# A fused spectral filter and token MLP: natural order in the first middle unit, the first token tile ahead, and MLP product tiles that open as banks come free

## The chip, the cores and the metric

The kernel runs on one core of a Trainium2 chip. The metric is device time in microseconds (us) of one execution; lower is better. PE is TensorE, DVE is VectorE, ACT is ScalarE, SP is the synchronising engine, which issues the transfers. PSUM is the memory that the matrix products write to; the kernel uses it in eight banks. A *hole* is time in which TensorE stands still and waits.

## The reference, cut to what matters

```python
def _layernorm(x, axis=-1, eps=1e-5): ...

def _A_ref(x, w_r, w_i):                       # global spectral filter
    X = rfft2(x.astype(float32), axes=(-2, -1)) * (w_r + 1j * w_i)
    return irfft2(X, s=(S, D)).astype(bfloat16)

def _B_ref(x, w1, b1, w2, b2):                 # MLP over the tokens
    u = gelu(einsum("bsd,sf->bdf", _layernorm(x), w1) + b1)
    return (einsum("bdf,fs->bds", u, w2) + b2).transpose(0, 2, 1)

h  = A_x + _A_ref(_layernorm(A_x), A_w_r, A_w_i)
h2 = h + _B_ref(_layernorm(h), B_w1, B_b1, B_w2, B_b2)   # S=2048, D=512, F=1376, bf16
```

## The kernel before

All Fourier transforms are matrix products. The program has three stages on TensorE. First come the forward products. In the middle, eight "units" each mix rows, multiply by the filter weights on DVE (`v`, tile `V`), and start the inverse. Last come 16 token tiles: inverse products `g2`, a copy from PSUM by ACT (`eo`, tile `EO`), the transform `g3`, three adds on DVE (`tl`, `th`, `h`, tiles `TT` and `H`), a square and a reciprocal root on ACT (`q`, `r2`, tiles `JK` and `r`), and a normalised tile on DVE (`hh`, tile `HH`). The first MLP layer has 11 product tiles of 16 products each, one for every token tile: `mm1_t_s2` needs `hh_s2`. The second layer (`mm2`) and the final adds follow, and need all of the first.

The order of the instructions and the use of the eight PSUM banks are made by a list scheduler inside the program when it is built. An operation takes part in the order by its readiness and its priority; lists called FRONT force the order of some. A group of matmuls that share a bank is a unit of a class; each class has a limit of open banks, and a unit that is not `early` may take a bank only when all its inputs are ready.

```python
FRONT = {
    "dve": """bn_0 ag_0 ... fs_13 fs_14 fs_15 ys_12 ys_14""",           # cut
    "act": """rs_0 fs_0 ... ys_11 ys_13 yh_150 yh_151""",               # cut
    ...}
K = Builder(nc, {"f1": 7, "f2": 2, "x": 2, "g1": 2, "g2": 2, "g3": 2, "mm1": 5, "mm1b": 6, "mm2": 8})
...
            if not u.early and any(remaining[x.idx] > inner[x.idx] for x in u.ops if x.pw):
                continue                                     # wait until all inputs are ready
...
def mm1(t, s2):
    Mt = NP if t < 10 else 96
    if t not in w1units:
        w1units[t] = PsumUnit("mm1" if t < 5 else "mm1b", 1, early=t < 5)
    mm(f"mm1_{t}_{s2}", lambda bank: ps[0:Mt, bank, :], W1[:, s2, t * NP:t * NP + Mt], HH[:, s2, :], w1units[t],
       s2 == 0, s2 == NS2 - 1, s2 == 0, 2 if t < 5 else 1, 512)

for s2 in range(NS2):
    unit = PsumUnit("g2", 1)
    ...                                                      # g2, eo, g3, tl, th, h, q, r2, hh
    for t in range(5):
        mm1(t, s2)
```

So in the kernel before only five product tiles can be worked on while tokens still arrive; the sixth may open only when all 16 normalised tiles exist. (In the built order just one product of the sixth stands ahead of the last token tile's first product.)

## Time and profile before

| | before |
|---|---|
| time, median of the 3 runs known when the prediction was made (lowest to highest); 133.91 with a fourth | 133.87 us (133.81 to 134.03) |
| profiled span | 132.2 us |
| PE busy | 123.3 us, 93% of the span |
| first token tile's MLP product | 45.88 us |
| last token tile's first MLP product | 69.03 us |
| last matmul starts | 128.48 us |
| from there to the end of the span | 3.69 us |

How to read it: from the last token tile on, TensorE has all its inputs and runs at its own rate, so the end is set by how much work is left when that tile arrives. Every first-layer product done earlier, in a hole, comes off the end with 0.216 us. The lines of the profile are in the prediction below.

### The profile page before, as it was taken

How to read it: one execution, taken by the hardware profiler on the slowest of the kernel's cores; microseconds unless marked ns; L12 is line 12 of the kernel's file. 1: busy time of each engine (PE TensorE's matmuls, PEld its weight loads, DVE VectorE, ACT ScalarE, POOL GpSimd, SP SyncE). 2: the span in 40 equal slices, each digit the busy share in tenths (PEclk: the TensorE clock that was granted, in tenths of full speed). 3: DMA queues.
4: the chain of work that ended last, by engine and by line, in shares of the span. 5: the costliest groups of instructions: out<-in, count | busy, mean ns of one | idle time of the engine just before them, and what ended most of it. 6: DMA issues, size and time to landing. Idle time of an engine off the chain costs nothing.

```text
span 132.2 us, 2004 instructions
## 1 busy us (share of the span) xinstructions
PE 123.3 (93%) x773; PEld 73.2 (55%) x773; DVE 70.5 (53%) x133; ACT 62.7 (47%) x144; POOL 10.7 (8%) x30
## 2 busy tenths in 40 slices
PE   6799989999979799999989999999999999999990
PEld 2145656878757455444334444456666666666650
DVE  0599978999973999999950000000332422423322
ACT  4299966789867999966699222222000000000000
POOL 0089900003000000000000000000000000000000
PEclk9999999999999999999999999999999999999998
DMA  3999999999999999980000000000112112121121
GB/s 110 340 401 388 303 291 295 297 215 332 394 418 416 410 413 413 386 208 31 0 0 0 0 0 0 0 5 0 40 40 79 40 40 79 45 75 44 40 79 40
DMA packets 16920, 22.16 MB, mean 168 GB/s; under 512 B 2736, under 2 KB 12720, under 8 KB 16912
## 3 DMA queue, kind: packets, MB, share of 16 engines
q1 hardware_dynamic: 16624, 21.52, 48.6%
q10 hardware_dynamic: 288, 0.52, 1.4%
q8 instruction: 6, 0.10, 0.3%
q14 instruction: 2, 0.02, 0.0%
HBM read 19.95 MB, written 2.10 MB: 167 GB/s over the span
## 4 chain that ended last, share of the span: by engine, by line
PE 60%; ACT 16%; DVE 16%; DMA 3%; issue 3%
PE ps L553 60%; ACT JK L571 5%; ACT Y L571 4%; DVE H L903 4%; DVE V L828 3%; DMA X<-in_A_x_dram 3%; ACT EO L571 3%; DVE HH L908 2%; ACT rs L571 2%; DVE TT L894 2%; DVE TT L896 2%; ACT r L571 2%; ACT FS L571 1%; DVE Y L744 1%; ACT PQ L571 1%
## 5 line engine op out<-in xcount | busy, mean ns | idle before, releaser
L553 PE MATMUL ps<-HH,W 128*128 128x512 bf16 (+1 forms) x176 | 41.0, 379 | 1.3 <-DVE HH L908 1.1
L553 PE MATMUL ps<-GT,W 128*128 128x512 bf16 (+1 forms) x176 | 38.2, 379 | 0.0
L933 DVE SCALAR_TENSOR_TENSOR OUT<-ps,B2f,H 128x512 bf16<-128x512 f32 x16 | 12.0, 750 | 48.7 <-PE ps L553 48.7
L553 PEld LDWEIGHTS ps<-GT,W 128*128 128x128 bf16 (+1 forms) x176 | 25.5, 145 | 12.6
L553 PEld LDWEIGHTS ps<-HH,W 128*128 128x128 bf16 (+1 forms) x176 | 17.1, 100 | 22.1 <-DVE HH L908 2.2
L828 DVE TENSOR_TENSOR V<-ps,W 128x2048 bf16<-128x2048 f32 (+1 forms) x8 | 15.7, 2017 | 0.4 <-PE ps L553 0.2
L571 ACT ACTIVATE GT<-ps,B1f 128x512 bf16<-128x512 f32 (+1 forms) x11 | 7.1, 688 | 14.6 <-PE ps L553 14.6
L571 ACT ACTIVATE JK<-H,nm 128x512 bf16<-128x512 bf16 x16 | 11.6, 726 | 3.4 <-DVE H L903 3.2
L682 DVE BATCH_NORM_STATS2 st<-X 128x6 f32<-128x512 bf16 x15 | 9.8, 665 | 3.6 <-DMA X<-in_A_x_dram 3.6
L903 DVE TENSOR_TENSOR H<-ps,TT 128x512 bf16<-128x512 f32 x16 | 10.9, 681 | 0.0
L571 ACT ACTIVATE PQ<-ps 128x512 bf16<-128x512 f32 (+1 forms) x16 | 9.1, 591 | 3.7 <-PE ps L553 3.6
L553 PE MATMUL ps<-EM,V 128*128 128x128 bf16 x128 | 9.6, 220 | 0.4 <-ACT PQ L571 0.3
L571 ACT ACTIVATE EO<-ps 128x512 bf16<-128x512 f32 x16 | 9.3, 600 | 0.9 <-PE ps L553 0.9
L648 PE MATMUL ps<-ZT 128*128 128x512 bf16 x21 | 7.6, 481 | 2.1 <-DVE ZT L591 1.2
L553 PE MATMUL ps<-FS,X 128*128 128x256 bf16 x64 | 8.6, 274 | 0.8 <-ACT FS L571 0.5
L571 ACT ACTIVATE CS<-ps 128x512 bf16<-128x512 f32 (+1 forms) x16 | 8.4, 577 | 1.6 <-PE ps L553 1.6
L553 PEld LDWEIGHTS ps<-EM,V 128*128 128x128 bf16 x128 | 7.8, 98 | 2.5 <-issue 1.3
L553 PE MATMUL ps<-EM,PQ 128*128 128x256 bf16 x64 | 8.6, 273 | 0.5 <-ACT PQ L571 0.5
L553 PE MATMUL ps<-EM,Y 128*128 128x256 bf16 x64 | 8.6, 273 | 0.4 <-DVE Y L744 0.4
L571 ACT ACTIVATE Y<-ps 128x512 bf16<-128x512 f32 (+1 forms) x15 | 7.9, 566 | 0.2 <-PE ps L553 0.2
L660 POOL TENSOR_SCALAR FS<-FP,rs 128x256 bf16<-128x256 bf16 x8 | 7.4, 937 | 6.7 <-ACT rs L571 6.4
L894 DVE TENSOR_TENSOR TT<-ps,X 128x256 f32<-128x256 f32 x16 | 6.7, 416 | 2.1 <-PE ps L553 2.1
(38 smaller groups left out, 77.9 us busy)
## 6 DMA issues: line engine op xcount, KB each, us to landing
W<-in_B_w_dram SPq DMA_DIRECT2D x8, 688.0 KB, 9.6
W<-in_B_w_dram SPq DMA_DIRECT2D x10, 512.0 KB, 17.0
out_dram<-OUT SPq DMA_DIRECT2D x16, 128.0 KB, 1.7
W<-in_A_w_r_dram SPq DMA_DIRECT2D x4, 257.0 KB, 5.2
W<-in_A_w_i_dram SPq DMA_DIRECT2D x4, 257.0 KB, 5.7
X<-in_A_x_dram SPq DMA_DIRECT2D x4, 256.0 KB, 5.0
X<-in_A_x_dram SPq DMA_DIRECT2D x2, 512.0 KB, 6.6
W<-in_A_w_r_dram SPq DMA_DIRECT2D x4, 192.8 KB, 4.5
```

The lines of the kernel that those rows point to most:

```text
L553: return K.op(name, "pe", lambda eng, bank: eng.matmul(outf(bank), lhsT, rhs, start=start, stop=stop), ins=ins or [lhsT, rhs], occ=occ, la ...
L571: return eng.activation(dst, s, func, **kw)
L648: return K.op(name, "pe", lambda eng, bank: eng.matmul(ps[:, bank, :], ZT[:, 0:NP], ZT[:, :], start=True, stop=True), ins=[ZT[:, :]], occ= ...
L660: dve(f"fs_{i}", lambda eng, bank: eng.tensor_scalar(FS[:, i, :, :], FP[:, i, :, :], rs, None, op0=ALU.mult), [FP[:, i, :, :], rs], [FS[:, ...
L682: dve(f"bn_{i}", lambda eng, bank, i=i, x=x: eng.bn_stats(ST[:, i, 0:6], x), [x], [ST[:, i, 0:6]], 512, prio=25)
L744: dve(name, lambda eng, bank: eng.tensor_copy(dst, src(bank)), [], [dst], n, unit=unit, prio=28, last=last)
L828: return eng.tensor_tensor(vout, s, win, ALU.mult)
L894: dve(f"tl_{s2}", lambda eng, bank, tt=tt, xl=xl: eng.tensor_tensor(tt[:, 0, :], ps[:, bank, 256:512], xl, ALU.add), [xl], [tt[:, 0, :]], ...
L896: dve(f"th_{s2}", lambda eng, bank, tt=tt, xh=xh: eng.tensor_tensor(tt[:, 1, :], xh, ps[:, bank, 256:512], ALU.subtract), [xh], [tt[:, 1, ...
L903: return eng.tensor_tensor(hs.rearrange("p (h d) -> p h d", h=2), e, tt[:, :, :], ALU.add)
L908: dve(f"hh_{s2}", lambda eng, bank, s2=s2, hs=hs: eng.tensor_scalar(HH[:, s2, :], hs, NM[:, s2:s2 + 1], R2[:, s2:s2 + 1], op0=ALU.add, op1 ...
L933: dve(f"fin{s2}", lambda eng, bank, dst=dst, bia=bia, hs=hs: eng.scalar_tensor_tensor(dst, ps[:, bank, :], bia, hs, op0=ALU.add, op1=ALU.add),
```

## The change

It has three parts, each of which can be undone alone. Part 1 gives the first middle unit its groups in natural order: two products of 1024 elements in place of four of 512, one ACT copy of 512 in place of one ACT and one DVE copy of 256, and filter weights loaded by ten transfers in place of eight. Part 2 forces the order of DVE and ACT at the start of the token stage so that the first tile is finished ahead of others, and gives the first eight inverse groups a bank class of their own (`g2a`). Part 3 lets the sixth and seventh product tiles open early, at low priority and from set times on, so that their products may fill holes.

```diff
 # part 1
-    return 4 * u + 2 * i + r
+    return g if u == 0 else 4 * u + 2 * i + r
...
-    add("W0", [NP, 2, 4, LW], bf, region(2 * 4 * LW * 2))
+    add("W0", [NP, 4, 2, LW], bf, region(2 * 4 * LW * 2))
...
-            if g0 == 0:
-                d = W0[0:NP:2, w, :, :].rearrange("p g l -> p (g l)")
-                lst.append(dma(f"ld_wp{ch}_{w}", ...))              # one load for both components
...
+                d = W[2 * comp::4, g0:g0 + ng, w, :] if g0 else W0[2 * comp::4, :, w, :]
+                lst.append(dma(f"ld_wp{ch}_{w}{comp}", ...))        # one load for each
...
-            split = u == 0
+            split = G == 0
...
-                for w in range(2):
-                    ...
-                    K.op(f"v_0_{i}{w}", "dve", tw, ..., occ=598.0, lat=720.0, ...)
+                ...
+                K.op(f"v_0_{i}", "dve", tw, ..., occ=1115.0, lat=1235.0, ...)
 # part 2
-        fs_9 ag_12 bn_13 ... fs_15 ys_12 ys_14""",
+        fs_9 ag_12 bn_13 ... fs_15 ys_12 ys_14
+        tl_0 th_0 h_0 tl_1 th_1 h_1 hh_0""",
-        rs_13 ys_9 ys_10 rs_14 ys_11 ys_13 yh_150 yh_151""",
+        rs_13 ys_9 ys_10 rs_14 ys_11 ys_13 yh_150 yh_151
+        eo_0 eo_1 eo_2 eo_3 eo_4 q_0 r2_0 eo_5""",
-        unit = PsumUnit("g2", 1)
+        unit = PsumUnit("g2a" if s2 < 8 else "g2", 1)
 # part 3
+MM1B_FROM = {5: 54000.0, 6: 62000.0}
-            w1units[t] = PsumUnit("mm1" if t < 5 else "mm1b", 1, early=t < 5)
+            w1units[t] = PsumUnit("mm1" if t < 5 else "mm1b", 1, early=t < 7)
-           s2 == 0, s2 == NS2 - 1, s2 == 0, 2 if t < 5 else 1, 512)
+           s2 == 0, s2 == NS2 - 1, s2 == 0, 2 if t < 5 else 1 if t < 6 else 0.5, 512, nb=MM1B_FROM.get(t, 0.0))
```

(Cut: the bodies of the loads and of the product's views, the entry `"g2a": 2` in the Builder's classes, and the argument `nb`, which passes the set time on.)

## The prediction

> **What bounds the kernel now.** I read the page's header and busy row first, then its chain, then the groups by line, then the busy time of each engine in five stretches, then the timelines of the seams.
>
> ```profile
> span 132.2 us, 2004 instructions
> ...
> PE 123.3 (93%) x773; PEld 73.2 (55%) x773; DVE 70.5 (53%) x133; ACT 62.7 (47%) x144; POOL 10.7 (8%) x30
> ...
> PE ps L553 60%; ACT JK L571 5%; ACT Y L571 4%; DVE H L903 4%; DVE V L828 3%; DMA X<-in_A_x_dram 3%; ACT EO L571 3%; DVE HH L908 2%; ACT rs L571 2%; DVE TT L894 2%; DVE TT L896 2%; ACT r L571 2%; ACT FS L571 1%; DVE Y L744 1%; ACT PQ L571 1%
> ```
>
> TensorE is busy 93% of the span and carries 60% of the chain. So the change can pay only by closing TensorE's idle time ahead of the long run of MLP products. The chain in order of time says where that run starts:
>
> ```profile
> 66.66 0.69 DVE H L903
> 67.35 0.33 DVE HH L908
> 67.68 0.05 issue
> 67.73 61.15 PE ps L553 x282
> 128.88 0.03 issue
> ```
>
> From 67.73 us on, 282 matmuls follow without a hole: 61.15/282 = 0.217 us each. They are 106 of the 176 first-layer products and all 176 of the second layer. Each product done before 67.73 takes 0.216 us off the end, if it fills a hole. The stretches (columns: length, then busy us of PE, weight loads, DVE, ACT, POOL, then clock and DMA) say how large the holes are:
>
> ```profile
> 18.00:22.67 4.67, 4.53 (x45) 2.87 (x46) 3.33 (x6) 3.06 (x7) 0.00 (x0) 1.00 1.21 293
> 22.67:38.60 15.93, 15.40 (x209) 12.26 (x206) 15.72 (x8) 12.85 (x25) 1.27 (x7) 1.00 1.03 324
> 39.80:54.50 14.70, 13.77 (x93) 8.59 (x94) 12.67 (x32) 13.85 (x36) 0.00 (x0) 1.00 1.03 414
> 54.50:69.00 14.50, 14.09 (x64) 5.84 (x62) 13.40 (x34) 10.78 (x30) 0.00 (x0) 1.00 0.35 95
> 69.00:128.90 59.90, 59.86 (x277) 35.60 (x276) 11.26 (x15) 7.94 (x12) 0.00 (x0) 1.00 0.10 33
> ```
>
> In the token-tile stage, 39.8 to 69, a busy interval overlaps the next issue and hides part of a hole. So I counted from start to start: a 512-column matmul has a 0.216 us slot, a 256-column one 0.109. What exceeds the slots is idle: 1.02 us ahead of the first MLP product, then 0.19, 0.08, 0.06, and near the end 0.20, 0.42 and 0.29 where tiles 12, 13 and 14 are late. **Sum 2.26 us.** The first hole and the tokens' start are these:
>
> ```profile
> 44.64 0.38 PE L553 MATMUL ps<-EO,IF 128*128 128x512 bf16 x1
> 45.88 0.38 PE L553 MATMUL ps<-HH,W 128*128 128x512 bf16 x1 [0.86 <-DVE HH L908]
> ```
>
> The first middle unit on DVE:
>
> ```profile
> 18.77 0.86 DVE L784 CAST CS<-ps 128x256 bf16<-128x256 f32 x2 [0.78 <-PE ps L553]
> 19.95 2.48 DVE L813 TENSOR_TENSOR V<-ps,W 128x512 bf16<-128x512 f32 x4 [0.32 <-PE ps L553]
> 22.67 2.29 DVE L828 TENSOR_TENSOR V<-ps,W 128x2048 bf16<-128x2048 f32 x1 [0.24 <-PE ps L553]
> ```
>
> Between 22.67 and 38.6 DVE is at 15.72 of 15.93 us and PE at 15.40: both are nearly full.
>
> **What the Trainium skill says.**
> - "TensorE: Matmul & The Clock Gate", section "Wait — 56ns, not 53.3ns?": a warm matmul issues every 215.7 ns at 512 columns and 55.6 at 128. The trace agrees: 0.216 and 0.056 us from start to start.
> - "VectorE: DVE Perf Modes", section "The TRN2 errata": an fp32 tensor_tensor takes (N+151)/0.96 ns. For N of 512, 1024 and 2048 that is 691, 1224 and 2291; the trace's product groups have 682, 1218 and 2284. It agrees, so fewer, larger products save the fixed part.
> - "PSUM — Partial Sum Buffer", section "PSUM bank collisions raise a hardware error": one semaphore guard per bank. The kernel does this, so a matmul's start can hang on the eviction of the bank's previous tenant. One such wait matters below.
> - "DMA: Bandwidth & Descriptors", Specifications: full rate needs at least 512 B a transfer. The new weight rows are 514 B, just above it.
>
> **Part 1: first middle unit.** Four products of 512 become two of 1024. On DVE, start to start: 4 x 0.60 + tail = 2.48 us before; 2 x 1.14 (the step between the two 1024 products at 37.34) + tail = 2.37 after, 0.1 to 0.2 us less. The second DVE cast (0.43) goes, and ACT does one 512 copy (0.6) in place of one of 256 (0.38). DVE could then start the second unit's product at 19.95 + 2.28 = 22.24 instead of 22.67. But that product waits for PE: in the changed order 23 first-stage matmuls, 16 half-row ones and two small ones precede its last input, against 25 and 16. That is -2 x 0.109 + 2 x 0.056 and one 0.09 stall less: 0.2 earlier, at 22.47. Then unit 2's inputs come later in PE's new order (after eight more inverse products and two whole first-stage tiles): I add the slots to 24.74, so unit 2's product starts at about 24.8, against 24.88 before. By unit 5 PE, which has issued the same work in both kernels, is the gate again. So this part keeps only the removed stall, **about 0.1 us**. The weights for unit 0 arrive as more, smaller transfers (10 issues in place of 8, rows of 514 B in place of 2056). They landed at 14.57 and are used at 19.95. Those of units 4 to 7 landed at 28.14, used at 29.28; a delay of some 0.25 us (263 KB at about 295 instead of 400 GB/s, both read from the page's GB/s row, an estimate) stays hidden.
>
> **Part 2: first token tile ahead.** DVE's forced order takes the first tile's final add ahead of the second tile's first add, and ACT does the square before the sixth copy. The add goes from 42.69 to about 42.47, the square from 43.81 to 43.21 (it was behind a copy), the normalised tile from 45.32 to 44.73, the first MLP product from 45.88 to about 45.25. With four more 256-column products ahead of it and one 512-column one behind it, the 1.02 hole becomes about 0.2. But the fifth tile's transform now stands after three MLP products and takes a bank that the eighth copy has to empty, and that copy ends at about 46.37: a new hole of about **0.5 us**, which the removed 0.19, 0.08 and 0.06 do not all repay. By the tenth transform I count 24 MLP products issued in 54.8 us against 20 in 54.5: 4 x 0.216 - 0.25 = **0.6 us** ahead.
>
> **Part 3: banks as they come free.** The sixth product tile may open while its inputs are still being made. The instruction order shows 11 of its products spread among the tiles from the tenth on, where there was one. They fill the holes of 0.20, 0.42 and 0.29 us: **0.9 us**. The transforms of tiles 14 and 15 come up to 0.9 us later on PE, which holds DVE's last tile by some 0.3 us, but its MLP products then stand at 69.7 on PE and their input is there by about 69.4: still no hole. The seventh tile's early permission is unused in the order.
>
> **Sum.** Products before the last tile's first: 86 against 76, so 10 x 0.216 = 2.16 us of work taken from behind; that tile starts at about 69.65 instead of 69.03, so 0.62 goes back. 2.16 - 0.62 = 1.54, with the 0.1 of part 1: 1.6 us. 133.87 - 1.6 = **132.3 us**, 1.2% less. All after is the same work at the same rate.
>
> **Rivals.**
> 1. *The gain is swallowed by the DVE and ACT chain.* DVE has 1.58 us a token tile (0.33 + 0.33 + 0.60 + 0.33 from start to start) and ACT is full from 42 to 55 (13.85 of 14.70). If fillers delay a transform that DVE waits for, tile 15 may come after 69.7 and a hole opens. For it: both are nearly full. Against it: by my count PE reaches that tile only at 69.65, later than its input. Then 0.5 to 1.0 us of gain: 132.9 to 133.4.
> 2. *The early bank wait is as costly as the hole it replaces.* If copy 8 is later still, part 2 gives nothing and only the late fillers count: about 133.0.
> 3. *The middle stage keeps its 0.2 to 0.4 us.* If unit 2 is not held by PE, DVE starts everything after that much earlier: 131.9.
> 4. *The smaller weight rows come too late* and unit 4 waits. Slack was 1.1 us against an estimated 0.25; if it happened, about 133.5.
>
> **Range and chances.** All holes together are 2.26 + 0.1 us, and 2% is 2.68 us: a clear win would need all of that and 0.3 us of rival 3 on top. A loss of 2% needs a wait that nothing in the profile announces. So 132.3, range 131.6 to 133.2; faster 0.04, same 0.95, slower 0.01.
>
> **What would show it right or wrong.** In the profile of the changed kernel: two 1024 products of about 1.22 us in the first unit; unit 1's product at about 22.5, unit 2's at 24.8; first MLP product at about 45.2 with a wait of under 0.4 us; a bank wait on a copy of about 0.5 us just after; no PE hole over 0.15 us between 56 and the end; the unbroken PE run starting at about 55 instead of 67.7. It is wrong if PE still waits for the normalised tiles after 60 us, if unit 4's product waits for a transfer, or if the last DVE tile moves beyond 69.7 us.

## The result, and the profile after

The changed kernel took 131.94 us (median of 4 fast runs, 131.87 to 132.05), the kernel before 133.91 in the same rounds (133.81 to 134.03). The ratio is 0.9853 with a 95% interval of 0.9836 to 0.987: 1.5% less, within the 2% that count as the same, as predicted; 132.3 was predicted and the range of 131.6 to 133.2 holds it. (A ratio is the mean time of one kernel's fast runs over that of the other's fast runs of the same rounds, so it is not quite the ratio of the medians quoted.)

The header and the busy row of the page, after:

```profile
span 130.2 us, 1995 instructions
...
PE 121.6 (93%) x763; PEld 73.6 (57%) x773; DVE 70.2 (54%) x130; ACT 62.8 (48%) x144; POOL 10.7 (8%) x30
```

One warning on reading it: the matmul count is x763, but the weight loads are x773 as before, and the program has 773 matmuls. Ten records are missing. Seven of them show in the chain of waits after, in order of time, as the "issue" steps of 0.05 us from 54.15 us on, most of them 10.8 us apart (the step at 46.20 is another thing, the way from a copy to the matmul that waited for it):

```profile
45.71 0.49 ACT EO L574
46.20 0.05 issue
46.25 7.90 PE ps L556 x47
54.15 0.05 issue
54.20 10.74 PE ps L556 x49
64.94 0.05 issue
64.99 10.74 PE ps L556 x49
...
121.62 5.59 PE ps L556 x25
127.20 0.02 issue
127.23 0.75 DVE OUT L931
```

At each of them two matmul starts lie 0.43 us apart in the trace, exactly two slots of 0.216: a matmul ran there whose record is gone, so this is no idle time. Read so, the chain has nothing but TensorE from 46.25 us to the last matmul; before, it went through DVE until 67.73.

The stretches answer to those of before (same columns; the ends of the first, third and last are set by each kernel's own times):

```profile
18.00:22.67 4.67, 4.58 (x49) 3.20 (x50) 3.04 (x4) 2.79 (x6) 0.00 (x0) 1.00 1.06 282
22.67:38.60 15.93, 15.18 (x204) 12.11 (x203) 15.56 (x8) 13.58 (x26) 1.27 (x7) 1.00 1.01 315
39.70:54.50 14.80, 14.17 (x95) 8.95 (x97) 12.79 (x32) 14.01 (x37) 0.00 (x0) 1.00 1.02 412
54.50:69.00 14.50, 14.45 (x68) 6.60 (x68) 13.25 (x34) 10.26 (x30) 0.00 (x0) 1.00 0.41 118
69.00:127.00 58.00, 57.73 (x265) 34.76 (x267) 11.48 (x16) 8.07 (x12) 0.00 (x0) 1.00 0.10 34
```

From 54.5 to 69 TensorE is busy 14.45 of 14.50 us (14.09 before), with 68 weight loads in place of 62: the late holes are closed. The first holes of the token stage, after (timeline of the seam, all engines, cut):

```profile
44.56 0.41 DVE L906 TENSOR_SCALAR HH<-H,nm,r 128x512 bf16<-128x512 bf16 x1
...
45.09 0.34 PEld L556 LDWEIGHTS ps<-HH,W 128*128 128x128 bf16 x3 [0.28 <-issue]
...
45.33 0.59 PE L556 MATMUL ps<-HH,W 128*128 128x512 bf16 x2 [0.25 <-DVE TT L894]
...
45.61 0.59 ACT L574 ACTIVATE EO<-ps 128x512 bf16<-128x512 f32 x1
...
46.25 0.39 PE L556 MATMUL ps<-EO,IF 128*128 128x512 bf16 x1 [0.33 <-ACT EO L574]
```

There are three weight loads for MLP products and only two matmul records: the first product is one of the missing ten. The next starts at 45.33, so the first started at about 45.12, one slot earlier, and the wait ahead of it is 0.2 us, not the 0.25 + 0.2 that the records suggest. Counted from start to start, the two holes are 0.20 and 0.49 us. (Some expectations below have 0.41 and 0.27 for them: the same sum, with the missing product put into the second hole.) The fifth tile's transform then waits for its bank until a copy (45.61 + 0.59 = 46.20) has emptied it.

The first middle unit on DVE, after:

```profile
18.72 0.42 DVE L783 CAST CS<-ps 128x256 bf16<-128x256 f32 x1 [0.78 <-PE ps L556]
19.91 2.36 DVE L811 TENSOR_TENSOR V<-ps,W 128x1024 bf16<-128x1024 f32 x2 [0.76 <-PE ps L556]
22.41 6.83 DVE L826 TENSOR_TENSOR V<-ps,W 128x2048 bf16<-128x2048 f32 x3
```

To compare profiled runs I take three marks from each trace. The first token data's arrival, a (start of the first statistics instruction on DVE), moves by up to 0.36 us from run to run whatever the kernel, and shifts everything after it; so the other two marks are counted from it. The *gate*, g, is the start of the last token tile's first MLP product; n is the number of products issued before it. The last matmul's start ends the compute, and the rest of the span is the *tail*. Since TensorE has no holes after the gate in any of these kernels, the gain in compute must be (n - 76) x 0.216 minus the delay of g - a. That sum agrees with the measured gain within 0.02 us in every trace, which is the check on the counts. (The 76 of the kernel before are 15 token tiles times five product tiles, and one product of the sixth.)

### The profile page after: what moved, and what is told of

Its sections match the earlier page's. It is cut to its first block, busy times and chain, and to the rows that moved or that the text cites. A ratio compares the mean times of both kernels' runs of the same rounds, so it can differ in the third digit from the quotient of the medians.

```text
span 130.2 us, 1995 instructions
## 1 busy us (share of the span) xinstructions
PE 121.6 (93%) x763; PEld 73.6 (57%) x773; DVE 70.2 (54%) x130; ACT 62.8 (48%) x144; POOL 10.7 (8%) x30
## 4 chain that ended last, share of the span: by engine, by line
PE 76%; ACT 12%; DVE 6%; DMA 3%; issue 2%
PE ps L556 75%; ACT Y L574 4%; DVE V L826 3%; DMA X<-in_A_x_dram 3%; ACT rs L574 2%; ACT JK L574 2%; ACT EO L574 2%; ACT FS L574 1%; DVE Y L743 1%; ACT PQ L574 1%; DVE OUT L931 1%; DVE st L681 1%; DVE FS L659 0%; PE ps L647 0%; ACT r L574 0%
## 5 line engine op out<-in xcount | busy, mean ns | idle before, releaser
L556 PE MATMUL ps<-HH,W 128*128 128x512 bf16 (+1 forms) x173 | 40.1, 380 | 0.4 <-DVE TT L894 0.2
L574 ACT ACTIVATE CS<-ps 128x512 bf16<-128x512 f32 (+1 forms) x16 | 8.9, 588 | 1.2 <-PE ps L556 1.2
L647 PE MATMUL ps<-ZT 128*128 128x512 bf16 x19 | 7.0, 487 | 2.3 <-DVE ZT L594 1.2
```

The source lines that it names most:

```text
L556: return K.op(name, "pe", lambda eng, bank: eng.matmul(outf(bank), lhsT, rhs, start=start, stop=stop), ins=ins or [lhsT, rhs], occ=occ, la ...
L574: return eng.activation(dst, s, func, **kw)
L647: return K.op(name, "pe", lambda eng, bank: eng.matmul(ps[:, bank, :], ZT[:, 0:NP], ZT[:, :], start=True, stop=True), ins=[ZT[:, :]], occ= ...
```

## The experiments

All twelve gave correct results. The column "ratio" is to the kernel before in the same rounds (its medians were 133.91 to 133.99). In the rounds of e5 to e8 one run of the kernel before, at 135.51, makes these four ratios about 0.001 too low; the medians are not touched by it. Each row's last five columns come from one profiled run.

| kernel | parts | median us | ratio (95%) | a | n | g - a | compute gain | tail |
|---|---|---|---|---|---|---|---|---|
| before | none | 133.91 | 1 | 4.72 | 76 | 64.31 | 0 | 3.69 |
| after | 1+2+3 | 131.94 | 0.9853 (0.9836 to 0.987) | 4.67 | 86 | 64.86 | 1.62 | 3.37 |
| e1_first_unit | 1 | 133.54 | 0.9966 (0.9954 to 0.9979) | 4.68 | 76 | 64.23 | 0.09 | 3.36 |
| e2_token_first | 2 | 133.95 | 0.9988 (0.9975 to 1.0001) | 4.97 | 76 | 64.22 | 0.09 | 3.70 |
| e3_early_banks | 3 | 133.01 | 0.9924 (0.9912 to 0.9935) | 4.63 | 83 | 64.92 | 0.91 | 3.70 |
| e4_no_first_unit | 2+3 | 132.57 | 0.9887 (0.9873 to 0.9901) | 4.95 | 86 | 64.98 | 1.50 | 3.69 |
| e8_no_fill | 1+2 | 133.39 | 0.9967 (0.992 to 1.0014) | 4.66 | 76 | 64.12 | 0.19 | 3.36 |
| e10_no_token_first | 1+3 | 132.73 | 0.9907 (0.9892 to 0.9921) | 4.96 | 83 | 64.82 | 1.01 | 3.36 |
| e6_hh0_first | all, other order | 132.37 | 0.9867 (0.9835 to 0.99) | 4.69 | 86 | 65.24 | 1.24 | 3.41 |
| e9_copy8_first | all, other order | 132.11 | 0.9858 (0.9842 to 0.9875) | 4.90 | 85 | 64.80 | 1.46 | 3.37 |
| e5_two_more_issues | none, 77 issues | 133.57 | 0.9959 (0.9926 to 0.9992) | 4.68 | 76 | 64.32 | -0.01 | 3.38 |
| e7_two_fewer_issues | all, 75 issues | 132.31 | 0.9867 (0.9834 to 0.99) | 4.60 | 86 | 64.85 | 1.62 | 3.71 |
| e12_one_more_issue | none, 76 issues | 133.95 | 0.9996 (0.9982 to 1.0011) | 4.67 | 76 | 64.35 | -0.04 | 3.71 |
| e11_after_four_more | all, 79 issues | 132.00 | 0.9861 (0.9831 to 0.9891) | 4.81 | 86 | 64.86 | 1.62 | 3.34 |

Two kernels whose compute engines have exactly the order of before (e5, e12) stand at -0.01 and -0.04, so a compute gain is good to about 0.04 us, and the 0.09 of e1 and e2 is not far above that.

My theory was the prediction's sum: each part closes its own holes, 0.1 + 0.6 + 0.9. The rivals were that a part's gain is waited away later (then part 2 alone gives nothing), that the middle stage keeps more than 0.1, and that something outside the token stage gives the rest.

### Each part alone

**e1_first_unit** is the kernel before with part 1 of the diff, no other line changed.

> Part 1 alone (first middle unit in group order with two products, its weight layout and loads), nothing of the token tiles. My theory: the middle stage keeps about 0.1 to 0.16 us (second-unit product near 22.4, unit 5's near 31.5 instead of 31.67), and the synchronising engine's program with two more transfer issues shortens the way from its last branch to its drain from 0.46 to about 0.17 us, another 0.3 us: total 0.45 us less than before. Rival: the short branch came with the finish time or by chance, then 0.1 to 0.2 us less and a branch gap of 0.46. Token-stage holes stay at 2.2 to 2.3 us.

It took 133.54 us against 133.99, 0.45 less (0.34% by the ratio of means). The trace splits this: the compute gained 0.09, the data arrived 0.05 earlier by chance, and the tail was 0.33 shorter. The page and the last step of the chain show the tail without any further counting. The last DVE operation ended at 129.52, 2.2 us ahead of the end of the span:

```profile
span 131.7 us, 1993 instructions
...
128.77 0.75 DVE OUT L929
```

Before, it ended at 128.90 + 0.75 = 129.65, 2.5 us ahead of 132.2:

```profile
128.90 0.75 DVE OUT L933
```

So what part 1 is worth in the middle stage is about the predicted 0.1, and the larger piece lies where the prediction had nothing; the expectation above has it because the trace of the changed kernel was known by then. The last experiments follow it up.

**e2_token_first** is the kernel before with part 2 alone.

> Part 2 alone (first token tile ahead, a bank class of its own for the first eight inverse transforms). My theory: the last tile's normalised input still comes at about 69 us and 76 products stand before it as in the kernel before, so what is won early is waited away later: 0.0 us, within 0.1; the hole before the first product falls from 1.02 to about 0.4, the holes at tiles 12 to 14 and 15 grow by the same sum. Rival, the additive reading of my prediction: 0.6 us less. Branch gap stays 0.46.

It took 133.95 us against 133.99, no difference that its six runs can tell from none. Its first hole is as short as in the changed kernel, and still nothing comes of it: TensorE now runs ahead and waits for the late tiles instead. The timeline of PE shows the two longest waits:

```profile
64.22 0.59 PE L555 MATMUL ps<-HH,W 128*128 128x512 bf16 x2
65.01 1.02 PE L555 MATMUL ps<-HH,W 128*128 128x512 bf16 x4 [0.20 <-DVE HH L910]
66.50 3.71 PE L555 MATMUL ps<-HH,W 128*128 128x512 bf16 x15 [0.47 <-DVE HH L910]
```

Counted from start to start, the holes ahead of tiles 11 to 14 are 0.28, 0.37, 0.42 and 0.29 us, against 0, 0.20, 0.42 and 0.29 before. (One record is missing here; the weight loads show that it is the last product ahead of the third of these holes, so that one is 0.42 and not 0.63.) So of the early holes some 0.6 us was closed (1.36 before, 0.77 here), and some 0.45 us opened again late. The last tile's gate is set by the chain on DVE, and that came only 0.09 us earlier.

**e3_early_banks** is the kernel before with part 3 alone.

> Part 3 alone (sixth product tile may open early). 83 products stand before the last tile's first, against 76. My theory: holes at tiles 12 to 14 (0.90 us) are filled, the early ones (1.36) stay: 0.9 us less than before, the last tile's first product near 69.65. Rival: without the early start, the fillers push transforms back and DVE's last tile after 69.7, then 0.5 us or less. Branch gap stays 0.46.

It took 133.01 us against 133.99 and gained 0.91 us of compute: 7 more products ahead of the gate (7 x 0.216 = 1.51) less a gate 0.61 later. There is no hole of the late kind left:

```profile
64.80 0.38 PE L554 MATMUL ps<-EO,IF 128*128 128x512 bf16 x1
65.02 5.34 PE L554 MATMUL ps<-HH,W 128*128 128x512 bf16 x24
```

The early hole of 1.02 us stays. The size for part 3 was right.

### The parts in pairs

**e4_no_first_unit** is the changed kernel with part 1 taken back.

> Parts 2 and 3 without part 1. My theory: 86 products before the last tile's first, which starts near 69.7: 1.5 us less than before, so more than parts 2 and 3 alone together if those are 0.0 and 0.9. It lacks part 1's 0.15 and, if the branch gap hangs on the synchronising engine's program, its 0.3 too: 132.4 us. Rival for the tail: 132.1 us with a short branch gap. Rival, additive: equal to the sum of parts 2 and 3 alone.

It took 132.57 us against 133.99: 1.50 us of compute, as expected, and the long tail of 3.69. (The time is 0.17 above the expected 132.4; in the profiled run the first data came 0.23 us later than in that of the kernel before.)

**e8_no_fill** is the changed kernel with part 3 taken back: `early=t < 5` again, and no third priority.

> The changed kernel without the early sixth tile (parts 1 and 2). My theory: the same 76 products ahead of the last tile as before, whose input comes at the same time, so it is worth what part 1 alone is, 0.45 us less than before, and 1.5 us slower than the changed kernel; late holes of about 1.2 us at tiles 11 to 14. Additive reading: 0.6 us less than part 1 alone, thus 1.05 us less than before.

It took 133.39 us against 133.96, with wide limits (one run at 134.74). The stretches tell most here:

```profile
39.70:54.50 14.80, 14.17 (x95) 8.95 (x97) 12.78 (x32) 14.00 (x37) 0.00 (x0) 1.00 1.02 411
54.50:69.00 14.50, 13.59 (x61) 5.48 (x61) 13.30 (x34) 10.78 (x30) 0.00 (x0) 1.00 0.39 112
```

Up to 54.5 us it is the changed kernel to the last digit of PE: 14.17 us, 95 matmuls, the early gain is there. In the next stretch PE has 13.59 us of work (up to 0.2 more with the missing record) where the changed kernel has 14.45, and before had 14.09: the gain of the first is waited away in the second. The four late holes are those of e2, 0.28, 0.36, 0.42 and 0.29 us, 1.35 in sum where 1.2 was expected.

**e10_no_token_first** is the changed kernel with part 2 taken back.

> The changed kernel without the first token tile ahead (parts 1 and 3). Theory that the three parts' sizes follow from products ahead of the last tile and its start: 83 products there as in part 3 alone, so part 3 alone (0.98) and part 1 alone (0.45) add up: 1.4 us less than before, 132.55 us, and 0.55 us slower than the changed kernel. So part 2 would be worth 0.55 beside part 3 and nothing without it.

It took 132.73 us against 133.94: 1.01 us of compute, 7 products moved. The time fell by 1.21 where 1.4 was expected. In the profiled run the first data came 0.24 us later than in that of the kernel before, which would be enough to explain it; that the other runs had the same delay is not shown.

Parts 1, 2 and 3 alone gain 0.09, 0.09 and 0.91. Parts 1 and 2 together give 0.19 and 1 and 3 give 1.01: these add up. Parts 2 and 3 together give 1.50, not 1.00. So part 2 is worth 0.1 alone and 0.6 beside part 3 (1.62 - 1.01 = 0.61 in the full kernel). The rival "waited away" holds for part 2 alone, and is wrong for the whole change, since part 3 gives PE the work with which to fill the waits.

### Two attempts to gain more

The changed kernel keeps three early holes (0.2, 0.5 and 0.1 us). Two versions tried to close them by another forced order.

**e6_hh0_first** normalises the first tile before the second tile's final add.

```diff
-        tl_0 th_0 h_0 tl_1 th_1 h_1 hh_0""",
+        tl_0 th_0 h_0 tl_1 th_1 tl_2 hh_0 h_1 th_2 tl_3 h_2 th_3 hh_1 h_3 ...""",
-        eo_0 eo_1 eo_2 eo_3 eo_4 q_0 r2_0 eo_5""",
+        eo_0 eo_1 eo_2 eo_3 eo_4 q_0 r2_0 eo_6 eo_5 q_1 eo_7 r2_1 eo_8 q_2 ...""",
```

> The changed kernel with the first tile's normalisation put ahead of the second tile's final add on DVE, and its root ahead of the seventh copy on ACT. The hole before the first MLP product (0.41 us) should close, as that input comes near 44.1 instead of 44.56; the fifth transform still waits for the eighth copy, so the second hole (0.27) may grow to 0.5. Theory that holes decide: 0.1 to 0.3 us faster than the changed kernel. Rival: DVE and ACT, which are full, lose as much on the second tile, and nothing or a loss is left.

It took 132.37 us, 0.4 more than the changed kernel (each against the kernel before of its own rounds, by the medians), so the theory missed. The normalised tile was indeed 0.3 us earlier and the first MLP product started at 44.96. But the fifth tile's transform came later:

```profile
44.26 0.41 DVE L906 TENSOR_SCALAR HH<-H,nm,r 128x512 bf16<-128x512 bf16 x1 [0.22 <-ACT r L574]
...
46.59 0.39 PE L556 MATMUL ps<-EO,IF 128*128 128x512 bf16 x1 [0.73 <-DVE H L901]
```

The scheduler gave this transform another bank, whose previous tenant is the third tile's transform, and DVE frees that only with the third tile's final add. The hole ahead of it is 0.89 us where the changed kernel has 0.5.

**e9_copy8_first** has ACT make the eighth copy before the second tile's square, so that the bank of the fifth transform is free sooner.

```diff
-        eo_0 eo_1 eo_2 eo_3 eo_4 q_0 r2_0 eo_5""",
+        eo_0 eo_1 eo_2 eo_3 eo_4 q_0 eo_6 r2_0 eo_5 eo_7 q_1 r2_1""",
```

> The changed kernel with the eighth copy put ahead of the second tile's square on ACT, to free the fifth transform's bank about 0.7 us earlier (copy at 44.9 instead of 45.6). The order of TensorE keeps the same place for the fifth transform. If that bank wait is what the 0.27 us hole is made of, the hole closes; the second tile's normalisation comes some 0.5 us later, and its first product (at 47.15 on TensorE, input ready at 46.9) may wait 0.2 to 0.4 us in turn. So 0.1 us faster to 0.2 us slower than the changed kernel; a gain of 0.3 would say that ACT had room, which I don't expect.

It took 132.11 us: no gain. The hole ahead of the transform did close (it started at 46.01), but one of 0.31 us opened just behind it, the square of the second tile came later, its product waited 0.41 us, and one product fewer (85) was done before the gate. In both attempts what one tile gained in the order another lost. ACT was busy for 14.0 of 14.8 us in the changed kernel; that this lack of slack is the reason is not tested, and in e6 the wait that decided was for a bank and DVE.

### The tail

Part 1 brings two more transfer issues: 77 in place of 75. Every trace with 75 issues has a tail of 3.69 to 3.71 us, and those of e1, e8, e10 and the changed kernel have 3.36 or 3.37. To see if the issues do it, and not the changed compute:

**e5_two_more_issues** is the kernel before, with two small bias loads cut into two transfers each. The order of every compute engine is the same instruction for instruction.

```diff
-    dma("ld_b1b", B1s[0:96, 10:11], ...)
-    dma("ld_b2", B2s[:, :], ...)
+    for k_, (r0, r1) in enumerate(((0, 64), (64, 96))):
+        dma(f"ld_b1b{k_}", B1s[r0:r1, 10:11], ...)
+    for k_ in range(2):
+        dma(f"ld_b2{k_}", B2s[64 * k_:64 * k_ + 64, :], ...)
```

> The kernel before with its two smallest bias loads cut in two each: two more transfer issues on the synchronising engine (77 instead of 75, as in the changed kernel), the same bytes, every compute engine's order unchanged. Theory of the program's length: the gap from that engine's last branch to its drain falls from 0.46 to about 0.17 us and the time by 0.3 us, to about 133.7. Rival (the short gap came from the weight layout or from finishing earlier): gap 0.46, no difference. A third way: two issues more cost something themselves, up to 0.1 us.

It took 133.57 us against 133.96 (one of the runs of before in these rounds was at 135.51, which moves the ratio and its interval and not the medians). The compute did not move (0.01 us); the last DVE operation ended 2.2 us ahead of the end of the span, not 2.5:

```profile
span 131.8 us, 1996 instructions
...
128.87 0.75 DVE OUT L937
```

**e7_two_fewer_issues** is the changed kernel with four constant loads joined into two, so that it has 75 issues again.

```diff
-    for h in range(2):
-        dma(f"ld_D2_{h}", ...)
-        dma(f"ld_IF_{h}", ...)
+    dma("ld_D2", EM[:, 2048:3072], cin["D2"][:, :], ...)
+    dma("ld_IF", IF[:, :, :], cin["IF"][:, :, :], ...)
```

> The changed kernel with four constant loads joined into two: 75 issues instead of 77, same bytes, compute orders unchanged. Theory of the program's length: gap back to about 0.46 us and 0.3 us slower than the changed kernel, about 132.3 us, while all products and holes stay as they are. Rival: gap 0.17 and 131.95 us.

It took 132.31 us, 0.37 more than the changed kernel's 131.94, with the same 1.62 us of compute gain and the tail of 3.71. So 0.3 us of the change's gain has nothing to do with its compute.

The last two runs asked how the number of issues matters.

**e12_one_more_issue** is the kernel before with only the second bias load cut, 76 issues.

> The kernel before with one bias load cut in two: 76 transfer issues on the synchronising engine, compute orders unchanged. The question is how its last stretch (0.465 us from its last branch to its drain with 75 issues, 0.168 with 77) depends on the number of issues. Theory 'gradual' (each further issue takes a share off): 0.31 us, time about 133.75. Theory 'threshold' (the code's length places the branch target on one or the other side of what has been fetched already): either 0.465 with the time of before (133.95), or 0.17 with about 133.6, nothing between. Expected: one of the two values, without knowing which.

**e11_after_four_more** is the changed kernel with both bias loads cut, 79 issues.

> The changed kernel with both bias loads cut in two: 79 issues, compute orders unchanged. Theory 'gradual': the last stretch falls further, below 0.168 us, and the time to 131.7 or less. Theory 'threshold': the stretch stays at 0.17 us and the time at 131.9 to 132.0; if the length matters in steps that come back, 0.465 and 132.3. Expected: 0.17 and no gain, so that no more is to be had from this.

With 76 the kernel before took 133.95 us, no gain; with 79 the changed kernel took 132.00, no further gain. So the effect comes in a step, between 76 and 77 issues, and is not gradual. But the expectation for 76 had the place wrong: the last stretch of SP, from branch to drain, is short there (0.16 us), and yet the tail is long, because the branch itself comes 0.38 us later. Put side by side, SP's last instructions in the traces show one pause that moves by one instruction for each issue (ordinary table, us from the last matmul's start; the wait is for the last store, whose last packet ends at 2.53 in all):

| issues, kernel | last issue ends | wait begins | wait ends | branch begins | drain begins | 8 KB instruction fetch recorded |
|---|---|---|---|---|---|---|
| 75, before | 1.53 | 1.57 | 2.90 | 2.95 | **3.42** | 3.98 |
| 76, e12 | 1.53 | 1.58 | 2.91 | **3.33** | 3.50 | 3.95 |
| 77, e5 | 1.53 | **1.96** | 2.92 | 3.00 | 3.17 | 2.73 |
| 77, after | 1.53 | **1.95** | 2.91 | 2.98 | 3.15 | 2.62 |
| 79, e11 | 1.53 | 1.59 | 2.90 | 2.95 | 3.12 | -2.17 |

The bold entry is the one that comes some 0.3 to 0.4 us later than in the other rows. With 75 issues the pause lies between branch and drain, with 76 between wait and branch; in both it is on the way to the end. With 77 it lies between the last issue and the wait, where SP would have stood waiting for the store anyway, and costs nothing. With 79 no such entry is late; if the pause moved on by the same rule, it stands ahead of the last but one issue, which waits for DVE anyway, and the fetch record that follows it lies there too, at -2.17, between the ends of the last but two (-3.23) and the last but one issue (-0.85). In each row the fetch record lies 1.0 to 1.2 us after the end of the instruction ahead of the pause (for 79 counted from -3.23). The Trainium skill, "Runtime: NRT & Kernel Launch", section "Instruction fetch mechanics", says that an engine's instruction memory is refilled in blocks and that crossing a block's boundary is mostly hidden. A boundary in SP's program at a fixed number of instructions fits all five rows; the crossing would then cost 0.3 to 0.4 us here and be hidden only where SP waits for something else. The branch's target, which the expectation for 76 blamed, is not the cause: with 76 and 77 issues the pause lies ahead of the branch. That the pause moves with the number of issues, and that the tail depends on what stands there, is shown for 75, 76 and 77; that it is the crossing of a block is inferred from the fetch record that comes with it, and stays open. In the rows with a visible pause that record begins only after the pause has ended (3.98 after 3.42), so it cannot be what SP waited for, and the trace does not name the engine that it belongs to.

## Why the prediction was right, point by point

**Range and sum.** The compute gain was 1.62 us where the sum said 1.6. The time fell by 1.97 (medians). The difference is 0.32 of tail (3.69 - 3.37) and 0.05 of earlier data in the profiled pair: 1.62 + 0.32 + 0.05 = 1.99, the difference of the two profiled spans. It took 131.94 and not 132.3 because of the tail. The third rival had named 131.9; that this number came is chance, since its cause (0.2 to 0.4 us kept in the middle stage) did not.

**"All after is the same work at the same rate."** This is the step that failed. It held for TensorE, but the end of the span is not TensorE's: SP's last instructions became 0.3 us quicker, since part 1's two extra transfer issues moved a pause into a wait. I had counted the issues ("10 issues in place of 8") and asked only if the data would come late.

**Part 1.** The step from the first token data to the first token tile's first add is 36.96 to 36.98 us in traces without part 1 and 36.86 to 36.88 in those with it: 0.1, as predicted. The products of 1024 took 1.22 us each. The second unit's product started at 22.41 (predicted 22.47), the third's at 24.75 (24.8). The last weights of units 4 to 7 landed at 28.67 us, 0.53 later than before where 0.25 was estimated, and were used at 29.16: not waited for, so the fourth rival is out, with half a us of slack left; the third (a gain of 0.2 to 0.4 here) is out too.

**Part 2.** Its steps came true nearly to the letter: the first normalised tile began at 44.56 (predicted 44.73), the first product at about 45.12 (45.25), a wait of 0.2 (0.2), then a bank wait on the eighth copy, which ended at 46.20 (46.37), with a hole of 0.49 (0.5). By the tenth transform, at 54.63 (54.8), 24 products were out. What was wrong is the bookkeeping: the 0.6 us was put down to part 2 as if it were additive. Alone it is 0.09 (e2), beside part 3 it is 0.6 (after less e10). The second rival, that the bank wait eats the part's gain, is not what happens in e2: there the late waits eat it.

**Part 3.** Predicted 0.9, measured 0.91 alone (e3). In the changed kernel the last tile's first product started at 69.53 (predicted 69.65), its input was finished at 69.22 (69.4): no hole, so the first rival, a hole at the last tile, is out. The holes of the token stage fell from 2.26 to 0.77 us (0.20, 0.49 and 0.08), and none is left after 49 us. The unbroken run of PE begins at 46.25 in the chain, earlier than the 55 that I named.

## What to carry to other kernels

Making a producer early pays only if the consumer's engine has other work for the time thus freed; judge such a change by the count of products ahead of the last gate, times the slot, less the delay of that gate. A forced order that closes one wait can hand out another PSUM bank, and the bank's last reader then decides (e6). Count what a change does to the engine that ends the program as well: here two transfer issues gave 0.3 us, which looked like a gain of the compute until the issues were changed alone.

## What the Trainium skill lacked or had wrong

- "Runtime: NRT & Kernel Launch", section "Instruction fetch mechanics": it calls the cost of a block's boundary mostly hidden and gives no time for the case where it is not. In these runs a pause that fits it cost SP 0.3 to 0.4 us, and 0.31 to 0.34 us of the kernel's tail where it fell after the last wait (75 or 76 issues) and not before it (77 and 79). The page speaks of refills of 16 KiB; the record beside this pause has 8192 bytes (records of 16384 are in the traces too, on another queue).
- "Perfetto Trace Analysis", section "Tensor Engine Instruction (MATMUL, LD_WEIGHTS)": it says that a matmul's start is recorded and its end is estimated, and the counting of holes from start to start rests on that. It does not say that records can be missing: 13 of the 14 traces have 763 of 773 matmul records with all 773 weight loads, at gaps of 0.43 us that look like holes of 0.2 us.
- No page has the variation of the first load: the first token data arrived between 4.60 and 4.97 us in 14 profiled runs, whatever the kernel, and moved all after it. Differences below 0.4 us between two profiled spans have to be counted from that arrival.
